# RetNet attention with a SwiGLU FFN on one core: first FFN products placed between two head pairs, and the chain of states read from PSUM

## The chip, the cores and the metric

The kernel runs on one core of a Trainium2 chip. The metric is the device time in microseconds (us). TensorE is called PE, its weight load PEld, VectorE DVE, ScalarE ACT, GpSimd POOL, SyncE SP.

## The reference

For 8 batches, 8 heads, 576 positions and a head size of 64, in fp32:

```python
scores = scale * np.matmul(q, k.transpose(0, 1, 3, 2))
Dmat = np.where(rel >= 0, gamma[:, None, None] ** rel[None, :, :], 0.0)
attn = np.matmul(scores * Dmat[None], v)                      # retention, one gamma per head
x = attn.transpose(0, 2, 1, 3).reshape(B * S, H * D)          # 4608 x 512
g = x @ w_gate;  val = x @ w_val                              # 512 x 1536
out = (g * (1.0 / (1.0 + np.exp(-g))) * val) @ w_out          # 1536 x 512
```

## The kernel before, in words

**Pairs.** The attention is worked off in 32 pairs of heads: 8 batches of 4 pairs (`HP` = 4). A pair's sequence is cut in 9 chunks of 64 positions. Retention is computed in the chunked way: inside a chunk by scores and a mask, across chunks by a state of 64 x 64 that is decayed and added to. The parts of a pair, with their lines before the change:

- `transposes` (L459): q and k turned so that PE can use them; by PE for pairs 0 to 3 (L471, L476), by DVE for the others (L489).
- `scores` (L561): products of k and q inside a chunk, L566 for the last chunk, L572 for the others, into PSUM. Pairs 0 to 3 put the last chunk's scores into bankE, the others into `sr`.
- `new_states` (L536): each chunk's own k-v products, L542, into PSUM `z`. Half `z[:, 0]` is for the even chunks, `z[:, 1]` for the odd.
- `masked` (L575): ACT copies `z[:, 0]` to `even` in SBUF (L583). DVE masks the scores (`own` L579, `last` L588). Then come the states, on DVE: `pairs` (L593) joins two chunks, `odd` (L598) is a chain of three steps in which each needs the one before, `evens` (L603) fills the states between.
- `own_values` (L523, products L531) and `earlier_values` (L545, products L554 and L558): scores times v and state times q, into PSUM `outer`.
- `to_x` (L608): DVE applies the last decay and writes the pair's quarter of x (L624, L648).

`scores` and `z` share the two banks of the tile `inner`.

**Order.** The order of every engine is written out by hand; the program is not rescheduled. For the first batch, `tick(t)` at t = 0 to 5 (L675 to L698) starts pair t, does scores and states of pair t - 1 and values of pair t - 2. Work on DVE and ACT of a pair is put in `pieces`, and `go_on` releases it.

**First tile.** The FFN's first tile has 512 tokens; its 12 blocks f of 128 hidden columns are made by `up0(f, chunks)` (L756, products L761, one gate and one value product for each quarter c of x, into bankA and bankB for even f, bankC and bankE for odd f). The weights come from HBM as 8-byte numbers and are turned into fp32 by `split` on ACT (L404, L405) and `rounding` on DVE (L418, L419). Each `rounding(j)` starts `split(j + 1)`, and some splits start the load of a later weight (`load_w`, L385 and L387; from the sixth on through ACT's queue). Before the change, ticks 4 and 5 are followed by `up0` for f = 0 and 1: quarters 0 and 1 after tick 4, quarters 2 and 3 after tick 5 (L1083 to L1085).

**Later tiles.** The other four tiles have 1,024 tokens and use sums and differences of blocks by a written table, so that fewer products are needed: `up_step` (L976, products L992) and `down_step` (L1030, products L1039). Their sums are spread over DVE and POOL: `reads` (L929) takes results out of the banks and sums them, `add` (L795) makes sums of x, of weights and of hidden blocks, L1013 to L1020 are the SwiGLU. Four banks take turns. Pairs 4 to 31 are done between these products: `tick` queues their DVE and ACT work as pieces, and every step releases one.

Of the kernel before, what the change touches and what calls it, by code (L numbers as in the profile page):

```python
# [17 lines left out]
ALU = mybir.AluOpType  # L18
# [136 lines left out]
def kernel(  # L155
# [32 lines left out]
    nc = tc.nc  # L188
# [5 lines left out]
    HP = H // 2  # L194
    L = D
    NC = S // L
    NFULL = S // P
# [29 lines left out]
    z = inner[:, :, 256:512].rearrange("p r (c d) -> p r c d", d=D)  # L227
# [21 lines left out]
    at = [4096 + 512 * i for i in range(4)] + [x0_at + 512 * i for i in range(4)]  # L249
# [14 lines left out]
    def whole(i):  # L264

        return i < needed(2) - 2
# [67 lines left out]
    step = tab[:, 2 * H : 2 * H + 2 * HP]  # L334
# [35 lines left out]
    halves = [(i, f) for f in range(2) for i in order[0:2]] + [(i, f) for i in order[2:] for f in range(2)]  # L370
# [18 lines left out]
    def bits_of(i, f):  # L389

        if i < NUP:
            return raws[i].rearrange("p c (f m two) -> p f c m two", f=2, two=2)[:, f]
        return raws[i].rearrange("p (f c) (d m two) -> p f (c d) m two", f=2, m=P, two=2)[:, f]

    def split(j):

        i, f = halves[j]  # L400
        bits = bits_of(i, f)
        top, ulp = [rest[:, part_at + 512 * (2 * n + j % 2) : part_at + 512 * (2 * n + j % 2 + 1)] for n in range(2)]
        blocks = lambda a: a.rearrange("p (c m) -> p c m", m=P)
        nc.scalar.activation(out=blocks(top), in_=bits[:, :, :, 1].bitcast(F32), func=AF.Prelu, scale=2.0 ** -112, alpha=2.0 ** 32)  # L404
        nc.scalar.activation(out=blocks(ulp.bitcast(I32)), in_=bits[:, :, :, 0].bitcast(U32), func=AF.Copy, scale=2.0 ** -29)  # L405
        parts[j] = top.bitcast(I32), ulp.bitcast(I32)
        m = j - 2 if 1 < j < 4 else j // 2
        if f and m != RAWS and m + RAWS + (m < RAWS) < len(order):
            load_w(m + RAWS + (m < RAWS))

    def rounding(j):

        i, f = halves[j]
        dst = weights[i][1][f].bitcast(I32)
        top, ulp = parts.pop(j)
        nc.vector.tensor_scalar(out=dst, in0=top, scalar1=3, scalar2=None, op0=ALU.logical_shift_left)  # L418
        nc.vector.tensor_tensor(out=dst, in0=dst, in1=ulp, op=ALU.add)  # L419
        if j + 1 < len(halves):  # L420
            split(j + 1)

    for f in range(2):
# [7 lines left out]
    even = const.tile([P, NFULL, D], F32, name="even")  # L431
# [8 lines left out]
    def places(i):  # L440
        return other if i < HP and i % 2 else (ret, ret_last, state)

    def last_scores(i):
        return bankE[:, 0:L] if i < HP else sr
# [10 lines left out]
    def vector(i):  # L455

        return i == 0
# [78 lines left out]
    def new_states(i):  # L536
        s = st[i]
        for c in range(NFULL):
            for r in range(2):
                for hl in range(2):  # L540
                    rows, at = chunk(i, hl, 2 * c + r)
                    nc.tensor.matmul(z[half[hl], r, c], s["kn"][chunk(i, hl, 2 * c + r, i < HP)], s["v"][rows, at],  # L542
                                     start=True, stop=True, skip_group_check=True)
# [31 lines left out]
    def masked(i):  # L575
        p, sr, (ret, ret_last, state) = i % HP, last_scores(i), places(i)

        def own():
            nc.vector.tensor_tensor(out=ret, in0=sc, in1=near[:, 2 * p : 2 * p + 2].unsqueeze(2).to_broadcast([P, 2, NFULL, L]),  # L579
                                    op=ALU.mult)  # L580

        def copies():
            (nc.vector.tensor_copy if vector(i + 1) else nc.scalar.copy)(out=even, in_=z[:, 0])  # L583

        odd_states = state[:, 1:].rearrange("p (c r) d -> p c r d", r=2)[:, :, 1]

        def last():
            nc.vector.tensor_tensor(out=ret_last, in0=sr, in1=last_near[:, p], op=ALU.mult)  # L588

        def pairs():  # L590

            at = odd_states
            nc.vector.scalar_tensor_tensor(out=at, in0=even, scalar=step[:, p : p + 1], in1=z[:, 1], op0=ALU.mult, op1=ALU.add)  # L593

        def odd():
            at = odd_states
            for c in range(1, NFULL):
                nc.vector.scalar_tensor_tensor(out=at[:, c], in0=at[:, c - 1], scalar=step[:, HP + p : HP + p + 1],  # L598
                                               in1=at[:, c], op0=ALU.mult, op1=ALU.add)

        def evens():
            at = state[:, 0 : NC - 1].rearrange("p (c r) d -> p c r d", r=2)
            nc.vector.scalar_tensor_tensor(out=at[:, :, 1], in0=at[:, :, 0], scalar=step[:, p : p + 1], in1=even,  # L603
                                           op0=ALU.mult, op1=ALU.add)

        return [copies, own, [last, pairs, odd, evens]]

    def to_x(i):  # L608
# [66 lines left out]
    def tick(t, lo=HP, hi=NP, spread=False, then=None):  # L675
        go_on(len(pieces))
        if hi == HP:

            if lo <= t - 1 < hi:
                scores(t - 1, True)  # L680
                new_states(t - 1)
                pieces.extend(masked(t - 1))
                go_on(3)
            if lo <= t - 2 < hi:
                own_values(t - 2)
            for f in transposes(t) if lo <= t < hi else ():
                f()
            if t + 1 == HP:
                split(0)
            if lo <= t - 2 < hi:  # L690
                earlier_values(t - 2)
                if t == HP:
                    rounding(2)
                    rounding(3)
                to_x(t - 2)[0]()
            if t + 1 == HP:
                rounding(0)
            return  # L698
        if lo <= t - 2 < hi:
            own_values(t - 2)  # L700
        if lo <= t - 1 < hi:
            new_states(t - 1)
        if lo <= t - 2 < hi:
            earlier_values(t - 2)
        if lo <= t - 1 < hi:
            scores(t - 1, t - 2 < lo)
        if lo <= t - 1 < hi and whole(t - 2) and not whole(t - 1):
            decay(slice(0, H), slice(0, H), half[1])
        copies, *masks = masked(t - 1) if lo <= t - 1 < hi else (lambda: None,)
        keys, *new = transposes(t) if lo <= t < hi else (lambda: None,)  # L710
        outputs = to_x(t - 2)[0] if lo <= t - 2 < hi else lambda: None
        late = needed(1) - 4 <= t < needed(1) - 2 or light(t - 2)
        if late and masks:
            own, (last, pairs, odd, evens) = masks
            pieces.extend([lambda: (copies(), own(), last(), outputs()), [pairs, odd, lambda: (evens(), keys())]])
        elif late:
            pieces.append(lambda: (copies(), outputs(), keys()))
        else:
            pieces.extend([lambda: (copies(), keys()), outputs])
            for own, (last, pairs, *rest_of) in [masks] if masks else []:  # L720
                pieces.extend([own, [lambda: (last(), pairs()), *rest_of]])
        if then and new:
            pieces.extend(new[:-1])
            pieces.append(lambda: (new[-1](), then()))
        else:
            pieces.extend(new)
            pieces.extend([then] if then else [])
        if not spread:
            go_on(len(pieces))
# [8 lines left out]
    def go_on(n):  # L738
        for _ in range(min(n, len(pieces))):
            while part_on():  # L740
                pass
# [14 lines left out]
    def up0(f, chunks):  # L756

        pair = banks[2 * (f % 2) : 2 * (f % 2) + 2]
        for gv, bank in enumerate(pair):
            for c in chunks:  # L760
                nc.tensor.matmul(bank, w_up[:, f // 4, gv, f % 4, c // 2, (c % 2) * P : (c % 2 + 1) * P], xs[0][:, c, :],  # L761
                                 start=(c == 0), stop=(c == HP - 1))
        if HP - 1 in chunks:
            s = io[:, (f % 2) * T0 : (f % 2 + 1) * T0]
            nc.scalar.activation(out=s, in_=pair[0], func=AF.Silu)
            nc.vector.tensor_tensor(out=hid0[f], in0=pair[1], in1=s, op=ALU.mult)
# [41 lines left out]
    for line in OUT_SUMS:  # L808
        i, s = line.split("|")
# [266 lines left out]
    for t in range(HP + 2):  # L1076
        tick(t, 0, HP)

        if t == 3:
            load(HP)  # L1080
        for j in {3: (1,), 5: (4, 5)}.get(t, ()):
            rounding(j)
        for f in range(2):  # L1083
            if t > 3:
                up0(f, range(2) if t == 4 else range(2, HP))  # L1085
    load(HP + 1)


# [116 lines left out]
```

## Time and profile before

| what | value |
|---|---|
| median of three runs (lowest, highest) | 1046.8 us (1046.59, 1056.34) |
| the profiled execution's own time | 1047.18 us |
| its span | 1045.5 us |
| busy: PE / PEld / DVE / ACT / POOL | 1027.6 / 843.9 / 653.9 / 297.2 / 401.9 us |
| DVE chain steps L598, 96 of them: min / median / max | 0.271 / 0.285 / 1.853 us |
| pair 2's values begin on PE (L531) | 27.65 us |
| last product of blocks 0 and 1 begins / block 2 begins on PE | 45.41 / 45.84 us |

A timeline line gives the start in us from the span's start, the length in us, the engine, the line of the kernel, operation and tiles, and in brackets the idle time before it with what ended it. A line of waits gives who waited for whom: us in total, times, longest. A line on a source line gives the number of instructions and the shortest, median and longest duration in ns. A line of windows gives a stretch, then its length and each engine's busy time, and at the end the granted clock of PE, the share of the DMA engines and GB/s.

### The profile page before, as it was taken

To read this page: it belongs to the slowest core of one execution; us is meant where nothing else is said; L and a number is where in the kernel's file an instruction comes from. 1 tells how busy PE (TensorE), PEld (TensorE's weight loads), DVE (VectorE), ACT (ScalarE), POOL (GpSimd) and SP (SyncE) were. 2 spreads that over 40 slices of the span, in tenths; PEclk is the share of its full clock that TensorE was granted. 3 is DMA by queue.
4 is the path that set the end of the run, shared out by engine and by line. 5 is a ranking of instruction groups with operands and counts; after the bars stand their busy time and mean duration, and the time that the engine had idled before them with its cause. 6 is when DMAs were issued, how large, how long until landed. Compare 5 with 4: busy or idle time off the path is not lost.

```text
span 1045.5 us, 21496 instructions
## 1 busy us (share of the span) xinstructions
PE 1027.6 (98%) x8448; PEld 843.9 (81%) x8448; DVE 653.9 (63%) x1063; ACT 297.2 (28%) x646; POOL 401.9 (38%) x347
## 2 busy tenths in 40 slices
PE   7999999999999999999999999999999999999998
PEld 6444555888888888888888888888888888888887
DVE  4678878777769757555357786535476644344644
ACT  3466423243533222232322102223120022231110
POOL 2002367767476035612223048312250483222505
PEclk9999999999999999999999999999999999999999
DMA  9999867776678887665676777545554565555653
GB/s 248 242 283 258 198 197 267 207 212 182 186 204 227 239 249 200 193 178 149 176 220 159 214 182 220 154 136 155 154 174 140 153 200 152 152 153 161 181 161 101
DMA packets 310380, 199.10 MB, mean 190 GB/s; under 512 B 220168, under 2 KB 254984, under 8 KB 310280
## 3 DMA queue, kind: packets, MB, share of 16 engines
q1 hardware_dynamic: 279000, 161.51, 57.2%
q10 hardware_dynamic: 31280, 36.22, 10.4%
q8 instruction: 67, 1.10, 0.5%
q14 instruction: 33, 0.27, 0.1%
HBM read 157.56 MB, written 40.11 MB: 189 GB/s over the span
## 4 chain that ended last, share of the span: by engine, by line
PE 76%; DVE 4%; DMA 1%; ACT 0%; issue 0%; POOL 0%; ACTq 0%; DVEq 0%
PE bankC L992 12%; PE bankE L992 12%; PE bankA L992 11%; PE bankB L992 11%; PE bankA L1039 6%; PE bankB L1039 6%; PE bankC L1039 6%; PE bankE L1039 6%; DVE rest L929 1%; PE outer L531 1%; PE inner L572 1%; DVE state L598 1%; PE outer L558 1%; PE inner L542 1%; DVE arena L1016 1%
## 5 line engine op out<-in xcount | busy, mean ns | idle before, releaser
L929 POOL TENSOR_TENSOR rest<-rest 128x512 f32<-128x512 f32 x65 | 92.1, 1421 | 296.7 <-DVE rest L929 277.9
L1013 ACT ACTIVATE io<-rest 128x256 f32<-128x256 f32 x180 | 74.9, 416 | 305.3 <-DVE rest L929 259.1
L992 PE MATMUL bankA<-rest,arena 128*128 128x256 f32 x544 | 128.9, 380 | 1.8 <-DVE rest L929 1.0
L992 PE MATMUL bankC<-rest,arena 128*128 128x256 f32 x544 | 129.2, 380 | 1.4 <-DVE rest L929 1.4
L795 POOL TENSOR_TENSOR arena<-arena 128x512 f32<-128x512 f32 (+1 forms) x72 | 112.5, 1574 | 38.3 <-DMA up<-arena 22.4
L992 PE MATMUL bankE<-rest,arena 128*128 128x256 f32 x512 | 121.4, 380 | 1.0 <-DVE rest L929 1.0
L992 PE MATMUL bankB<-rest,arena 128*128 128x256 f32 x512 | 121.2, 379 | 0.0
L992 PEld LDWEIGHTS bankA<-rest,arena 128*128 128x128 f32 x544 | 103.0, 190 | 16.9 <-issue 1.9
L1020 POOL TENSOR_TENSOR arena<-rest,io 128x256 f32<-128x256 f32 x72 | 52.1, 729 | 167.3 <-ACT io L1013 167.3
L992 PEld LDWEIGHTS bankC<-rest,arena 128*128 128x128 f32 x544 | 102.8, 190 | 16.3 <-issue 1.8
L992 PEld LDWEIGHTS bankE<-rest,arena 128*128 128x128 f32 x512 | 97.0, 190 | 14.7 <-DVE rest L929 1.4
L992 PEld LDWEIGHTS bankB<-rest,arena 128*128 128x128 f32 x512 | 97.0, 190 | 13.4 <-issue 0.2
L795 POOL TENSOR_TENSOR rest<-rest 128x256 f32<-128x256 f32 (+1 forms) x66 | 67.8, 1048 | 100.9 <-DVE rest L419 61.2
L929 DVE TENSOR_TENSOR rest<-bankB,rest 128x512 f32<-128x512 f32 x72 | 48.8, 686 | 65.6 <-PE bankB L992 49.7
L929 DVE TENSOR_TENSOR rest<-bankC,rest 128x512 f32<-128x512 f32 x72 | 48.9, 687 | 64.6 <-PE bankC L992 45.9
L929 DVE TENSOR_TENSOR rest<-bankA,rest 128x512 f32<-128x512 f32 x72 | 48.8, 685 | 61.1 <-PE bankA L992 43.5
L929 DVE TENSOR_TENSOR rest<-bankE,rest 128x512 f32<-128x512 f32 x71 | 48.2, 687 | 60.5 <-PE bankE L992 46.1
L1016 DVE SCALAR_TENSOR_TENSOR arena<-rest,io 128x256 f32<-128x256 f32 x84 | 57.8, 689 | 11.1 <-ACT io L1013 10.9
L1039 PE MATMUL bankC<-arena 128*128 128x256 f32 x252 | 58.4, 381 | 0.3 <-issue 0.3
L1039 PE MATMUL bankB<-arena 128*128 128x256 f32 x252 | 58.3, 381 | 0.0
L1039 PE MATMUL bankA<-arena 128*128 128x256 f32 x252 | 58.0, 380 | 0.2 <-DVE arena L795 0.2
L1039 PE MATMUL bankE<-arena 128*128 128x256 f32 x252 | 57.9, 379 | 0.0
(189 smaller groups left out, 1632.4 us busy)
## 6 DMA issues: line engine op xcount, KB each, us to landing
arena<-up SPq DMA_DIRECT2D x234, 256.0 KB, 2.7
arena<-dn SPq DMA_DIRECT2D x104, 384.0 KB, 3.9
up<-arena ACTq DMA_DIRECT2D x78, 256.0 KB, 4.1
dn<-rest SPq DMA_DIRECT2D x78, 128.0 KB, 1.9
out_dram<-rest SPq DMA_DIRECT2D x31, 256.0 KB, 3.7
qk<-in_q_dram SPq DMA_DIRECT2D x108, 72.0 KB, 2.4
qk<-in_k_dram SPq DMA_DIRECT2D x108, 72.0 KB, 3.1
rest<-in_moe_w_out_dram ACTq DMA_DIRECT2D x6, 1024.0 KB, 5.4
```

The source lines that it names most:

```text
L531: m = nc.tensor.matmul(value(i, hl, c), s["v"][rows, at], ret[rows, c % 2 if whole(i) else hl, c // 2], start=start, stop=start, skip_grou ...
L542: nc.tensor.matmul(z[half[hl], r, c], s["kn"][chunk(i, hl, 2 * c + r, i < HP)], s["v"][rows, at], start=True, stop=True, skip_group_check= ...
L558: nc.tensor.matmul(xr[half[hl]] if c + 1 == NC else value(i, hl, c), state[half[hl], c, :], s["qT"][half[hl], column(i, hl, c)], start=Fal ...
L572: nc.tensor.matmul(sc[chunk(i, hl, 2 * c + r)[0], r if whole(i) else hl, c], kT[half[hl], at], qT[half[hl], at], start=True, stop=True, sk ...
L598: nc.vector.scalar_tensor_tensor(out=at[:, c], in0=at[:, c - 1], scalar=step[:, HP + p : HP + p + 1], in1=at[:, c], op0=ALU.mult, op1=ALU.add)
L795: eng.tensor_tensor(out=dst, in0=srcs[0], in1=srcs[1], op=ALU.add if op[0] == "add" else ALU.subtract)
L929: eng.tensor_tensor(out=at(op[1]), in0=at(op[2]), in1=at(op[3]), op=ALU.add if op[0] == "add" else ALU.subtract)
L992: m = nc.tensor.matmul(b[:, gv * TB : (gv + 1) * TB], w[:, gv, ts(c, P)], rhs[:, c, :], start=(opens and gv == 0 and c == 0), stop=(c == 1 ...
L1013: nc.scalar.activation(out=s, in_=src[:, 0:TB], func=AF.Silu, scale=-1.0 if negative else 1.0)
L1016: return lambda: nc.vector.scalar_tensor_tensor(out=dst, in0=src[:, TB : 2 * TB], scalar=-1.0, in1=s, op0=ALU.mult, op1=ALU.mult)
L1020: nc.gpsimd.tensor_tensor(out=dst, in0=src[:, TB : 2 * TB], in1=s, op=ALU.mult)
L1039: nc.tensor.matmul(b[:, m * TB : (m + 1) * TB], lhs[:, qd, ts(m, P)], w[:, qd], start=(opens and qd == 0 and m == 0), stop=(qd == NQ - 1), ...
```

## The change

Two things are changed. In the first batch, `tick(4)` no longer begins with scores and states of pair 3. It begins with the values of pair 2; then come block 0's products on quarters 0 and 1, pair 2's way into x, roundings 2 and 3 (the latter without starting split 4), then scores and states of pair 3, split 4, and block 1's products on quarters 0 and 1. After tick 5 both blocks take quarter 2 first, and then both take quarter 3.

For pairs 4 to 31 the chain of states reads PSUM: `pairs` writes only the first joined state to SBUF and joins the other three in place in `z[:, 1]`; `odd` takes its second input from `z[:, 1]`, and `evens` takes it from `z[:, 0]` in place of `even`. Pairs 0 to 3 keep the old form.

```diff
-    def rounding(j):
+    def rounding(j, ahead=True):
...
-        if j + 1 < len(halves):
+        if ahead and j + 1 < len(halves):
             split(j + 1)
...
+        firsts, summed = (NFULL, odd_states) if i < HP else (1, z[:, 1])
...
         def pairs():
-            at = odd_states
-            nc.vector.scalar_tensor_tensor(out=at, in0=even, scalar=step[:, p : p + 1], in1=z[:, 1], op0=ALU.mult, op1=ALU.add)
+            for at, c in ((odd_states[:, :firsts], slice(0, firsts)), (summed[:, firsts:], slice(firsts, NFULL))):
+                if firsts < NFULL or c.start == 0:
+                    nc.vector.scalar_tensor_tensor(out=at, in0=even[:, c], scalar=step[:, p : p + 1], in1=z[:, 1, c],
+                                                   op0=ALU.mult, op1=ALU.add)
         def odd():
             at = odd_states
             for c in range(1, NFULL):
                 nc.vector.scalar_tensor_tensor(out=at[:, c], in0=at[:, c - 1], scalar=step[:, HP + p : HP + p + 1],
-                                               in1=at[:, c], op0=ALU.mult, op1=ALU.add)
+                                               in1=summed[:, c], op0=ALU.mult, op1=ALU.add)
         def evens():
             at = state[:, 0 : NC - 1].rearrange("p (c r) d -> p c r d", r=2)
-            nc.vector.scalar_tensor_tensor(out=at[:, :, 1], in0=at[:, :, 0], scalar=step[:, p : p + 1], in1=even,
+            nc.vector.scalar_tensor_tensor(out=at[:, :, 1], in0=at[:, :, 0], scalar=step[:, p : p + 1], in1=even if i < HP else z[:, 0],
                                            op0=ALU.mult, op1=ALU.add)
...
-            if lo <= t - 1 < hi:
+            def new_pair():
                 scores(t - 1, True)
                 new_states(t - 1)
                 pieces.extend(masked(t - 1))
                 go_on(3)
+            if lo < t < hi:
+                new_pair()
             if lo <= t - 2 < hi:
                 own_values(t - 2)
...
                 earlier_values(t - 2)
                 if t == HP:
-                    rounding(2)
-                    rounding(3)
+                    up0(0, range(2))
                 to_x(t - 2)[0]()
+            if t == HP:
+                rounding(2)
+                rounding(3, False)
+                new_pair()
+                split(4)
+                up0(1, range(2))
...
+    for c in range(2, HP):
         for f in range(2):
-            if t > 3:
-                up0(f, range(2) if t == 4 else range(2, HP))
+            up0(f, [c])
```

## The prediction

> **What bounds the kernel now.** I read the page's busy shares first, then the list of waits by engine, then the timelines at the places that this list names, and last the durations of the lines that the diff edits.
>
> ```profile
> PE 1027.6 (98%) x8448; PEld 843.9 (81%) x8448; DVE 653.9 (63%) x1063; ACT 297.2 (28%) x646; POOL 401.9 (38%) x347
> q8 instruction: 67, 1.10, 0.5%
> ```
>
> TensorE (PE) is busy for 98% of the span. No PE product is added or removed, so all that the change can win or lose at first hand is time in which PE stands still. The waits of PE, in us (total, times, longest), those that this change can touch:
>
> ```profile
> PE bankC L476 <- issue: 1.7, 1, 1.7
> PE bankC L992 <- DVE rest L929: 1.4, 1, 1.4
> PE bankA L992 <- DVE rest L929: 1.0, 1, 1.0
> PE bankA L761 <- DVE rest L624: 0.5, 1, 0.5
> PE outer L531 <- DVE arena L418: 0.4, 1, 0.4
> ```
>
> Two groups. L476, L531 and L761 lie in the first 46 us, where the order is changed. The two L992 waits lie at 269 and 324 us, in the first full FFN tile. Nothing above 2 us is to be had at one place.
>
> The early stretch, timeline of PE and DVE (start, length, work, idle before):
>
> ```profile
> 21.49 0.27 PE L476 MATMUL bankC<-ident,rest 64*64 64x64 f32 x1
> 23.41 0.39 PE L476 MATMUL bankC<-ident,rest 64*64 64x64 f32 x6 [1.65 <-issue]
> ...
> 25.52 1.28 DVE L624 TENSOR_TENSOR rest<-outer,tab 128x256 f32<-128x256 f32 x3
> 27.65 1.01 PE L531 MATMUL outer<-ret,v 64*64 64x64 f32 x32 [0.38 <-DVE arena L418]
> ```
>
> The stop at 21.76 to 23.41 is in the middle of one group of products, with no wait of the program. The PE instructions from 23.41 to 27.65 number 254, and two of its sequencer: 256. A packet of the instruction queue is 1.10 MB / 67 = 16.4 KB, and 16,896 PE instructions over 66 packets are 256 each. The packets begin at 20.76 and 25.07 us, and each stop ends 2.6 us after such a start. I read both stops as PE waiting for its own next instructions while short 64x64 products use them up; the name DVE L418 at the second is then not the cause (what pair 2's values need of DVE, the last L624, ends at 26.80). The clock answers to the first stop:
>
> ```profile
> 23.75:27.16 3.41, 3.41 (x123) 3.33 (x117) 1.72 (x5) 2.69 (x6) 0.45 (x1) 0.50 1.08 284
> ```
>
> Column PEclk is 0.50 there and 1.00 around it. Last, the two later waits, DVE's timeline ahead of each, and the durations of the chain's line:
>
> ```profile
> 264.33 0.68 DVE L929 TENSOR_TENSOR rest<-bankB,rest 128x512 f32<-128x512 f32 x1
> 264.93 2.75 DVE L598 SCALAR_TENSOR_TENSOR state<-state,tab 128x64 f32<-128x64 f32 x3
> 267.61 1.27 DVE L929 TENSOR_TENSOR rest<-bankA,rest 128x512 f32<-128x512 f32 x2
> ```
>
> ```profile
> 319.05 3.29 DVE L598 SCALAR_TENSOR_TENSOR state<-state,tab 128x64 f32<-128x64 f32 x3
> 322.27 1.28 DVE L929 TENSOR_TENSOR rest<-bankC,rest 128x512 f32<-128x512 f32 x2
> ```
>
> ```profile
> L598 DVE SCALAR_TENSOR_TENSOR state<-state,tab x90: 271/285/1853, 11.9 to 778.6; 128x64 f32<-128x64 f32 x90
> ```
>
> Three chain steps of 0.285 us median (0.93 us together when undisturbed) take 2.75 and 3.29 us, and the readings of the banks, queued behind them on DVE, come late: PE stands until each is done. POOL runs an L795 or L963 operation under each slow step.
>
> **What the Trainium skill says.** "SBUF — State Buffer", section "Who interferes with whom": a VectorE instruction with two SBUF inputs contends with a GpSimd instruction that reads SBUF, one with at most one SBUF input outside the two-port modes does not. The trace agrees: L598, both inputs in SBUF, ranges from 271 to 1853 ns; L593, whose second input is in PSUM, from 465 to 472 ns over 30. "TensorE: Matmul & The Clock Gate", section "Part 1: The HAM clock gate (the "warmup" mystery)": the PE clock is halved after an idle window of about 3.4 us and restored after a busy one; windows are free-running. The trace agrees, with one half-clock window of 3.41 us after a stop of 1.65 us.
>
> **The change part by part.**
>
> (a) Chain of states, 28 pairs (i >= 4); pairs 0 to 3 keep their instructions. Removed: SBUF as second input of L598 and L603. Added: one DVE instruction a pair, since L593 (0.47 us at 256 columns) becomes one of 64 columns to SBUF and one of 192 that writes PSUM in place. By columns between the rows of 64 (0.285) and 256 (0.471): 0.285 + 0.41 = 0.69, so +0.22 us of DVE a pair, 28 x 0.22 = 6.2 us. No row of before shows DVE writing PSUM: between 0 and 0.5 us a pair; I take 0.22, and what hides it is DVE's idle 37%. Saved: the L598 steps that are above 0.38 us sum to 18 us of excess over 0.285; DVE is some 12 us less busy. On PE's path only two excesses count. At 264.93 the excess is 1.8 us, less 0.2 added: PE's 1.04 us vanish. At 319.05 it is 2.4 us: PE's 1.44 us vanish. Sum -2.48. What is late next: at 274.4 PE waits 0.51 us for kT (DVE L489); DVE comes about 1.6 us earlier there and PE 1.04, so this wait does not grow; I book no gain.
> New wait: the products L542 of the next pair overwrite z, which now is held until the last step (evens) rather than until pairs. Behind L542 on PE stand the earlier values, L558, which wait for the same evens in before too, and no PE wait at L558 or L542 is listed: cost 0; if that cover fails, L542's 0.5 us a pair is exposed.
>
> (b) First batch. Scores and states of pair 3 (L566, L572, L542; 136 instructions, 25.3 to 27.26, 1.95 us at the low clock) leave the place ahead of pair 2's values. So PE now reaches these values at 25.4 and waits for the last L624: start at 26.9, instead of 27.65 in before (-0.75). The instruction limit is no longer in the way: values of pair 2 are also 136 instructions, so the fetched block's edge falls behind them. Then: values of pair 2; block 0's four products (8 x 0.43 = 3.45); pair 3's scores and states, 1.1 at full clock (60 rows of the same kind in 1.2 at 59.66); block 1's four products, 3.45; values of pair 3, 1.5; eight products in quarters, 8 x 0.86 = 6.87.
> At full clock: 26.9 + 1.5 + 3.45 + 1.1 + 3.45 + 1.5 + 6.87 = 44.8, before 45.84: -1.0.
> But PE is now idle for 1.5 of the 3.41 us of the window 23.75:27.16, much as in the window before, which had 52% of work and was followed by the half clock. If the half clock stays to 30.58, values of pair 2 take 2.2 (to 29.1), and of the block's 3.45 only 0.74 is done by 30.58, so it ends at 33.3; the rest adds to 46.2: +0.35. Both ends: -1.0 and +0.35. I take +0.3, since the trace's own 52% window went to the half clock.
> DVE in this order: to_x(1) to 26.8, roundings 0 and 1 to 29.27, to_x(2) to 30.8, roundings 2 and 3 to 33.2, then pair 3's mask, last, pairs, chain, evens (2.5 us) after PE's 33.0 to 34.4. Block 1's second bank (bankE) must wait for `last`, which reads it: done 1.2 us after the states, while bankC's products take 1.72. The values of pair 3 need evens about 3.1 us after the states, and PE reaches L558 5 us after. Third-quarter products need to_x(2) only; the fourth, 3.4 us later, needs to_x(3), 1.5 us: PE's 0.47 us at L761 vanishes, as counted. Splits 4 and 5 on ACT stand behind the copy of pair 3's states, so the one weight load that ACT issues at 34.84 goes out 1 to 2.5 us later; ACT uses that slot at 58.4, and roundings are 5 us ahead of PE (done 54.5, used at 59.7): cost 0. The queues of SP and POOL keep their order.
>
> Sum: +0.3 - 2.5 = -2.2 against the profiled execution's 1047.18 us (span 1045.5 and 1.7 around it): 1045.0. That execution is 0.4 above the median of the runs, 1046.8, so I forecast **1044.6**.
>
> **The rivals.**
> 1. *Given back.* POOL's locks strike other DVE work of two SBUF inputs (L795, L929, L1016, which I saw at 1.4 to 2.0 us), or PE waits at kT instead; the first batch comes out at +0.75 more because the release at 27.65 was a true wait for DVE. For: 1.0 us of PE idle at 192.84 has such an L795 of 1.75 us. Against: those stay as they were. Half of (a), and +1.0: 1046.8 - 1.2 + 1.0 = 1046.6.
> 2. *More.* The clock comes back early (-1.0 in place of +0.3) and the 0.5 at kT goes: 1044.6 - 1.3 - 0.5 = 1042.8.
> 3. *Slower.* Steps that read and write PSUM are slow, or z held longer stops PE's L542 once a pair. From 0.09 us a pair on PE (2.5 / 28) the gain is gone; at the full 0.5 us, 28 x 0.5 - 2.2 = +11.8: 1058.6. Against: L593 with a PSUM input costs 0.471, L603 without one 0.479, and L558's cover.
> 4. *It does nothing:* the locked steps were late anyway, PE's waits stay with other names: 1046.8 + 0.3 = 1047.1.
>
> **How the numbers follow.** Forecast 0.55 (own range 1043.6 to 1045.7), rival 1 0.20, rival 2 0.12, rival 3 0.06, rival 4 0.07. About 1%, 10.5 us, is what a measurement of this kernel can tell from no change. The range 1041.8 to 1047.4 holds the first two rivals, the fourth and the forecast, and leaves out most of rival 3 and tails. Only rival 3 at its full price passes 1%: slower 0.03; nothing known makes 10 us of gain: faster 0.02; same 0.95.
>
> **What would show it.** Right: chain steps all near 0.28 us with no long ones; no PE wait near 269 and 324; L531 of pair 2 at 26.9 behind a named DVE L624; PE reaching f = 2 between 44.8 and 46.2. Wrong: PE waits at L542 or L558 for DVE; an in-place step over 0.6 us; new PE waits of over 1 us at L992.

## The result, and the profile after

The changed kernel takes 1043.54 us (median of 20 runs, 1040.74 to 1048.88), beside 1047.6 us for the kernel before in the same measurement (20 runs, 1044.41 to 1056.34). The medians are 4.1 us apart. The ratio worked out from all the runs is 0.9957, 95% interval 0.9942 to 0.9972, which is 4.5 us less, between 2.9 and 6.1. The forecast was 1044.6 us, 2.2 us less. The profiled execution of the changed kernel is a short one: its own time is 1040.84 us, its span 1039.1 us.

The first part of the profile's page, busy time by engine:

```profile
PE 1025.6 (99%) x8448; PEld 843.2 (81%) x8448; DVE 642.3 (62%) x1091; ACT 297.4 (29%) x646; POOL 400.5 (39%) x347
```

DVE has 28 instructions more and is 11.6 us less busy. The largest waits of PE, as listed for before:

```profile
PE outer L531 <- DVE rest L627: 1.8, 2, 1.5
PE bankE L1003 <- DVE rest L940: 0.9, 1, 0.9
...
PE bankA L772 <- issue: 0.4, 1, 0.4
```

(L1003 is before's L992, L772 its L761, L940 its L929.) Both waits of 1.0 and 1.4 us for a bank that L929 had not yet read are gone, and so are the wait of 0.5 us at kT and the stop at L476. A wait of 1.5 us at L531 is new. DVE's timeline at the place of the 3.29 us chain, and the durations of the chain's lines:

```profile
315.02 0.68 DVE L940 TENSOR_TENSOR rest<-bankB,rest 128x512 f32<-128x512 f32 x1
315.62 0.90 DVE L601 SCALAR_TENSOR_TENSOR state<-state,tab,inner 128x64 f32<-128x64 f32 x3
316.44 1.28 DVE L940 TENSOR_TENSOR rest<-bankC,rest 128x512 f32<-128x512 f32 x2
```

```profile
L595 DVE SCALAR_TENSOR_TENSOR inner<-even,tab,inner x28: 422/423/423, 61.3 to 769.0; 128x192 f32<-128x192 f32 x28
```

```profile
L601 DVE SCALAR_TENSOR_TENSOR state<-state,tab,inner x84: 269/281/283, 61.8 to 770.1; 128x64 f32<-128x64 f32 x84
```

The chain takes 0.90 us where it took 3.29. Of its 84 steps with an input in PSUM none is over 283 ns. POOL still works under it:

```profile
315.55 1.27 POOL L974 TENSOR_TENSOR arena<-arena 128x512 f32<-128x512 f32 x1
```

What held the steps before is seen by laying POOL's timeline of the kernel before beside the chain:

```profile
319.23 1.27 POOL L963 TENSOR_TENSOR arena<-arena 128x512 f32<-128x512 f32 x1
320.45 1.81 POOL L795 TENSOR_TENSOR arena<-arena 128x768 f32<-128x768 f32 x1
```

The two long steps begin at 319.39 and 320.62 and last 1.19 and 1.73 us, 0.9 and 1.4 us more than the median. They end at 320.58 and 322.35, each 0.08 us after one of these operations. This is so throughout. In the profile of the kernel before, 21 steps of the chain begin under a TENSOR_TENSOR of POOL (two tensor inputs) that has more than 0.32 us to go, and all 21 end 0.08 us after it. But 7 steps begin under a TENSOR_SCALAR of POOL (one tensor input), and all 7 end before it does. Over the fourteen profiles that are compared below, it is 175 of 175 steps with both inputs in SBUF under the one kind, and 0 of 79 under the other. In the changed kernel 22 of the 84 steps with a PSUM input begin under a TENSOR_TENSOR, and none is held. A chain of the kernel before, and the POOL operation under its last two steps, which take 0.40 and 0.28 us:

```profile
162.80 1.04 DVE L598 SCALAR_TENSOR_TENSOR state<-state,tab 128x64 f32<-128x64 f32 x3
163.05 0.85 POOL L793 TENSOR_SCALAR rest<-rest 128x256 f32<-128x256 f32 x1
```

The Trainium skill's "SBUF — State Buffer", "Who interferes with whom", says that a VectorE instruction with two SBUF inputs contends with a GpSimd instruction that reads SBUF. These traces agree for GpSimd's two-input operations, and do not show it for the one-input ones.

### The profile page after: what moved, and what is told of

The parts are those of the page before. It is cut to its first block, busy times and chain, and to the rows that moved or that the text cites. A ratio compares the mean times of both kernels' runs of the same rounds, so it can differ in the third digit from the quotient of the medians.

```text
span 1039.1 us, 21528 instructions
## 1 busy us (share of the span) xinstructions
PE 1025.6 (99%) x8448; PEld 843.2 (81%) x8448; DVE 642.3 (62%) x1091; ACT 297.4 (29%) x646; POOL 400.5 (39%) x347
## 4 chain that ended last, share of the span: by engine, by line
PE 78%; DVE 2%; issue 1%; ACT 0%; DVEq 0%
PE bankC L1003 13%; PE bankE L1003 13%; PE bankB L1003 13%; PE bankA L1003 13%; PE bankB L1050 6%; PE bankC L1050 6%; PE bankA L1050 6%; PE bankE L1050 6%; PE outer L531 1%; PE inner L572 1%; PE outer L558 1%; PE inner L542 1%; DVE rest L806 1%; DVE arena L806 0%; DVE rest L940 0%
## 5 line engine op out<-in xcount | busy, mean ns | idle before, releaser
L940 POOL TENSOR_TENSOR rest<-rest 128x512 f32<-128x512 f32 x65 | 91.6, 1414 | 299.1 <-DVE rest L940 279.8
L1003 PE MATMUL bankC<-rest,arena 128*128 128x256 f32 x544 | 129.1, 380 | 0.0
L1003 PE MATMUL bankA<-rest,arena 128*128 128x256 f32 x544 | 128.7, 379 | 0.0
L1003 PE MATMUL bankE<-rest,arena 128*128 128x256 f32 x512 | 121.4, 380 | 0.9 <-DVE rest L940 0.9
L1003 PE MATMUL bankB<-rest,arena 128*128 128x256 f32 x512 | 121.2, 379 | 0.0
L1003 PEld LDWEIGHTS bankA<-rest,arena 128*128 128x128 f32 x544 | 103.2, 190 | 14.5 <-issue 0.5
L1003 PEld LDWEIGHTS bankC<-rest,arena 128*128 128x128 f32 x544 | 102.9, 190 | 14.6 <-POOL arena L806 0.3
L1003 PEld LDWEIGHTS bankE<-rest,arena 128*128 128x128 f32 x512 | 96.9, 190 | 14.6 <-DVE rest L940 1.4
L1003 PEld LDWEIGHTS bankB<-rest,arena 128*128 128x128 f32 x512 | 97.1, 190 | 13.3
L940 DVE TENSOR_TENSOR rest<-bankB,rest 128x512 f32<-128x512 f32 x72 | 48.9, 687 | 67.4 <-PE bankB L1003 51.5
L940 DVE TENSOR_TENSOR rest<-bankC,rest 128x512 f32<-128x512 f32 x72 | 48.9, 687 | 65.8 <-PE bankC L1003 47.1
L940 DVE TENSOR_TENSOR rest<-bankA,rest 128x512 f32<-128x512 f32 x72 | 48.9, 687 | 61.5 <-PE bankA L1003 44.1
L940 DVE TENSOR_TENSOR rest<-bankE,rest 128x512 f32<-128x512 f32 x71 | 48.2, 687 | 60.0 <-PE bankE L1003 46.7
```

Source lines behind the costliest of these rows:

```text
L940: eng.tensor_tensor(out=at(op[1]), in0=at(op[2]), in1=at(op[3]), op=ALU.add if op[0] == "add" else ALU.subtract)
L1003: m = nc.tensor.matmul(b[:, gv * TB : (gv + 1) * TB], w[:, gv, ts(c, P)], rhs[:, c, :], start=(opens and gv == 0 and c == 0), stop=(c == 1 ...
```

## The experiments

Each stands with what was expected of it before it ran. Ratios are to the kernel before in the same measurement, with the 95% interval.

**The order alone** (the changed kernel with `masked` as before):

```diff
-        firsts, summed = (NFULL, odd_states) if i < HP else (1, z[:, 1])
...
-                                               in1=summed[:, c], op0=ALU.mult, op1=ALU.add)
+                                               in1=at[:, c], op0=ALU.mult, op1=ALU.add)
...
```

> Only the order of the first batch is changed; the chain of states is that of before. My theory (the order is worth 0 to 2 us, the chain the rest): ratio to before between 0.998 and 1.000; block 2 begins on PE at 44.0 to 46.2 us; the long L598 steps of up to 1.8 us and PE waits of 1.0 to 1.4 us behind them near 265 and 320 us are still there. Rival (the order carries the whole gain): ratio about 0.996, and PE's later waits are not larger than in the changed kernel.

Measured: 1.0006 (0.9992 to 1.0021). The later waits of PE are all there:

```profile
PE bankC L999 <- DVE rest L936: 2.1, 1, 2.1
PE outer L531 <- DVE rest L623: 1.9, 2, 1.5
PE outer L558 <- DVE state L602: 1.6, 1, 1.6
PE inner L542 <- ACT kn L506: 1.3, 2, 1.1
PE bankA L999 <- DVE rest L936: 1.3, 1, 1.3
```

Block 2 begins at 41.77 us, earlier than both ends of the expectation, and yet nothing is left at the end. The order does not carry the gain.

**The chain alone** (the kernel before with the new `masked`):

> Only the chain of states is changed; the first batch has the order of before. My theory: all chain steps near 0.28 us, no PE wait near 265 and 320 us, ratio 0.996 to 0.998 (2.5 to 4 us). Block 2 begins at 45.8 us as in before if the half clock and PE's stop at 21.8 us come in every execution; near 44 us if they come only in some. Rival (the order carries the gain): ratio 0.999 to 1.001.

Measured: 0.9945 (0.9926 to 0.9965), 5.8 us less. No PE wait near 265 or 320 us. It carries the whole gain. The gain is larger than expected (0.9945 against 0.996 to 0.998), and above the prediction's 2.5 us for the chain even at the interval's end of 3.7.

**The same instructions, but the chain's second input in SBUF** (chain alone, with the joined states written in place into `even`). It asks whether the memory of this one input is what counts:

```diff
-        firsts, summed = (NFULL, odd_states) if i < HP else (1, z[:, 1])
+        firsts, summed = (NFULL, odd_states) if i < HP else (1, even)
```

> First batch as in before. Pairs 4 to 31 have the split joining and evens from PSUM as in the changed kernel, but the three joined states are written in place into the SBUF tile even, so that each chain step again has two SBUF inputs. My theory [...]: long steps of 0.6 to 1.9 us come back, PE waits of about 1 us behind them too, ratio 0.999 to 1.002. Rival (the split, or another length of the steps, or z being used longer makes the gain): steps near 0.28 us and ratio 0.996 to 0.998.

Measured: 0.9997 (0.9981 to 1.0014). DVE's timeline at the same chain, and two of PE's waits:

```profile
320.29 3.24 DVE L602 SCALAR_TENSOR_TENSOR state<-state,tab,even 128x64 f32<-128x64 f32 x3
323.46 1.27 DVE L933 TENSOR_TENSOR rest<-bankC,rest 128x512 f32<-128x512 f32 x2
```

```profile
PE bankC L996 <- DVE rest L933: 1.5, 1, 1.5
PE bankA L996 <- DVE rest L933: 1.0, 1, 1.0
```

This kernel has the split, the in-place write and the evens from PSUM, and only lacks the PSUM input of the three steps. Without it the held steps are back (27 over 0.4 us, up to 1.85), and the whole gain is gone. So the gain comes from the memory of this one input; that `evens` reads PSUM is not what saves the time.

**Empty instructions ahead of the first transposition:**

> The kernel before, with 64 empty instructions for TensorE ahead of its first transposition, where it waits 4 us for data anyway. My theory (PE's stops in the first 30 us are at the edges of fetched blocks of 256 of its instructions): the stops move 64 instructions up in the program: the one at 27.65 us no longer stands at the first L531 of pair 2 but inside pair 3's scores or states (L572 or L542), and the one at 21.8 us no longer in the transposition of the last chunks (L476) but in L471 or L531 ahead of it. Rival (a wait for DVE or ACT): both stay at the same products.

This told nothing of its question: the program that was built holds 21,496 instructions as before, so the empty ones had been left out. It serves as a second execution of the kernel before: stops at L476 (0.2 us) and L531 (2.1 us), 1043.8 us in its single run.

**Real instructions ahead of it** (the same, with 16 products into a corner of PSUM that nothing reads):

```diff
+    for _ in range(16):
+        nc.tensor.matmul(outer[half[0], 1, 384 : 384 + L], ident[half[0], half[0]], ident[half[0], half[0]],
+                         start=True, stop=True, skip_group_check=True)
     for t in range(HP + 2):
         tick(t, 0, HP)
```

> The kernel before with 16 small products (64 instructions of PE) into an unused corner of PSUM ahead of the first transposition, where PE waits for data. My theory (PE stops at the edges of blocks of 256 of its instructions until the next block is fetched): the stops move 64 instructions up in the program, from L476 of pair 3 to pair 2's states or the first L531 of pair 1, and from the first L531 of pair 2 to the first L542 of pair 3, and each ends 1.3 to 1.6 us after a packet of the instruction queue does. Rival (a wait for DVE): the wait stays at the first L531 of pair 2.

PE's timeline:

```profile
19.97 0.28 PE L542 MATMUL inner<-v,rest 64*64 64x64 f32 x3 [0.82 <-issue]
...
25.34 0.69 PE L542 MATMUL inner<-v,rest 64*64 64x64 f32 x32 [1.97 <-issue]
25.86 1.33 PE L531 MATMUL outer<-ret,v 64*64 64x64 f32 x32
```

Both stops are at the products named, 64 instructions further up in the program, and the L531 of pair 2 no longer waits. The packets of the instruction queue end at 18.58 and 24.20 us, 1.4 and 1.1 us ahead; the second is a little under the span on record. (The one run of this kernel took 1052.5 us; with other stops in it, its time is not compared.) At the edges where before, after, chain_sbuf and nops_first stop, PE goes on 1.35 to 1.6 us after a packet's end. PE stops for its own instructions there; the name that the list of waits gave, DVE L418, was not the cause.

**The changed kernel again, and two variants** measured beside it:

> The changed kernel as it is, a second measurement beside the next two. If the chain carries all of the gain and the order none: ratio to before 0.994 to 0.997, the same as the kernel with the chain alone. If the order has a cost or a gain of its own: apart from that kernel's 0.9945 by more than 0.002.

Measured: 0.9956 (0.9941 to 0.9972), as the first time and as the chain alone.

The chain alone with only the quarter order of the diff:

```diff
-            if t > 3:
-                up0(f, range(2) if t == 4 else range(2, HP))
+            if t == 4:
+                up0(f, range(2))
+    for c in range(2, HP):
+        for f in range(2):
+            up0(f, [c])
```

> The new chain, the order of before, and of the new order only that blocks 0 and 1 both take quarter 2 before they take quarter 3. PE's wait of 0.47 us at L761 for the last quarter of x goes; nothing else changes. Ratio 0.994 to 0.996; 0.5 us is below what the runs can tell, so the profile decides: no wait at the up0 products of quarter 3, block 2 0.5 us earlier after the same start of pair 2's values.

Measured: 0.9961 (0.9946 to 0.9976). The wait of 0.47 us at quarter 3 is gone. Block 2 begins at 46.53, because PE's stop at L531 was 3.1 us in this execution, and the clock was halved for 6.83 us from 25.99 us on. So the half microsecond can't be read off block 2's start.

Pair 4's keys on GpSimd, in the changed kernel (`1 < i <= HP` for `1 < i < HP` in `keys`):

> The changed kernel with one thing moved: the keys of pair 4 are scaled by GpSimd in place of ScalarE. Theory A (the early time that the order wins is lost at pair 4's states, L542, which wait for the scaled keys, queued on ScalarE behind splits that wait for a weight from HBM): no wait at L542 of pair 4, block 4 begins 8.2 us after block 3 also where block 3 begins before 49 us, ratio up to 0.002 below that of the changed kernel. Theory B (the order wins nothing early, or the weight load itself is the limit): PE waits at a block's product for a rounding instead, block 4 not before 59 us, ratio that of the changed kernel.

Measured: 0.996 (0.9942 to 0.9978). No wait at L542, but block 3 began at 50.59 us, so the case that it was meant for did not come up. The run doesn't tell theory A from B.

**Where the order's early time goes.** In the profile of the changed kernel taken again, PE stands 2.16 us at L558. DVE's timeline ahead of it, then PE's:

```profile
163.78 0.88 DVE L806 TENSOR_TENSOR rest<-rest 128x256 f32<-128x256 f32 x1 [3.77 <-DMA dn<-rest]
164.59 0.27 DVE L595 SCALAR_TENSOR_TENSOR state<-even,tab,inner 128x64 f32<-128x64 f32 x1
```

```profile
166.71 1.13 PE L558 MATMUL outer<-qT,state 64*64 64x64 f32 x32 [2.16 <-DVE state L606]
```

The states stand on DVE behind a sum that waits for its buffer to be stored. Four kernels try this, with two mends: the states ahead of the sums, and the keys as above. They are the changed kernel with the first mend alone, the changed kernel with both, the order alone with both, and the kernel before with both as the measure for the last. The first mend, in the changed kernel:

```diff
             tick(tick_at[m], HP, FIRST, tick_at[m] + 1 < needed(1))
-            go_on(1)
+            go_on(2)
```

> The changed kernel, but while the first tile's down products run, pairs 10 to 12 have their states (joining, chain, evens) on VectorE ahead of the sums of down weights that stood between the mask and them. Theory A (the stop of 1.6 to 2.2 us at L558 near 165 us, seen in two of four executions with the new order, is these states waiting behind a sum whose buffer is still being stored): no PE wait at L558 there in any execution, no half-clock window near 166 us, median 0.5 to 1.5 us below that of the changed kernel. Theory B (the stop comes from the transfers, wherever the states stand): PE waits near 165 us as before, same ratio as the changed kernel's 0.9956.

The first mend alone measured 0.995 (0.9932 to 0.9968). No wait at L558, but PE now waits twice near 190 us, 0.9 and 1.0 us, where the changed kernel waited once. Its time cannot be told from the changed kernel's.

> As the last, and pair 4's keys scaled by GpSimd. If the order wins some 2.4 us in the first 45 us and loses them at pair 4's states and at 165 us: ratio 0.993 to 0.995, block 4 begins 8.2 us after block 3, no PE wait at L558. If not: 0.9956 as the changed kernel.

Both mends in the changed kernel: 0.9965 (0.9951 to 0.9978). Not faster; the expectation of 0.993 to 0.995 fails.

> The order of the first batch alone with the old chain, and the two mends (states ahead of the sums, pair 4's keys on GpSimd). If the order's early gain is real and was lost at these two places: ratio to the next kernel about 0.998 (2 us), to before 0.997 to 0.999. If the order wins nothing: the same time as the next kernel.

The order alone with both mends: 0.9996 (0.9981 to 1.0011).

> The kernel before with the same two mends, the measure for the last. The mends are for stops that executions of the order of before did not show: ratio 0.999 to 1.001.

The kernel before with both mends: 0.9995 (0.9978 to 1.0012). So with the two places mended the order still gains nothing, and my account of where its early time was lost is too narrow. The profile of the order with both mends shows a third place. ACT's timeline, then DVE's, then PE's waits:

```profile
54.54 0.67 ACT L404 ACTIVATE rest<-rest 128x512 f32<-128x512 f32 x1 [10.39 <-DMA rest<-in_moe_w_gate_dram]
```

```profile
55.24 0.43 DVE L418 TENSOR_SCALAR arena<-rest 128x512 int32<-128x512 int32 x1 [8.96 <-ACT rest L404]
...
60.44 0.73 DVE L489 STREAM_TRANSPOSE kT<-qk 128x576 f32<-128x576 f32 x1
```

```profile
PE outer L566 <- DVE kT L489: 4.1, 2, 3.6
```

ACT waits for a weight from HBM until 54.5 us. Splits, rounding and, behind them on DVE, pair 4's transposition wait for it, and PE's scores wait for that.

## Why the prediction was right, and where its sum was off

To see where each part's time comes from, the fourteen profiled executions are cut at four places on PE, with the lines named as in the kernel before. Each column is the length, in us, of the stage that ends there: the first batch with blocks 0 and 1, the rest of the first tile, the first up products of the later tiles, and all the rest.

| execution | to block 2 | to first L992 | to first L1039 | to PE's end |
|---|---|---|---|---|
| before | 45.8 | 130.2 | 151.1 | 714.4 |
| nops_first | 43.1 | 130.2 | 151.1 | 713.9 |
| edges | 45.1 | 132.7 | 156.1 | 713.0 |
| chain_sbuf | 47.8 | 130.2 | 150.5 | 713.7 |
| before_kept | 46.1 | 130.8 | 154.9 | 713.9 |
| chain_only (new chain) | 44.7 | 130.2 | 147.2 | 714.8 |
| chain_quarters (new chain) | 46.5 | 130.2 | 147.1 | 715.4 |
| order_only (new order) | 41.8 | 136.0 | 153.1 | 713.3 |
| order_kept (new order) | 43.1 | 134.0 | 152.7 | 713.9 |
| after (both) | 44.0 | 130.2 | 147.7 | 713.4 |
| after_again (both) | 42.8 | 136.4 | 148.0 | 713.7 |
| keys_pool (both) | 43.7 | 130.2 | 147.2 | 713.2 |
| states_first (both) | 42.5 | 132.1 | 149.3 | 714.5 |
| both_mended (both) | 46.1 | 130.2 | 148.1 | 714.9 |

- **Bound and places: right.** PE sets the time, and the chain's steps held by GpSimd made it stand. The third column is 152.8 on average for the seven executions with a chain in SBUF (150.5 to 156.1) and 147.8 for the seven with PSUM (147.1 to 149.3): 5.0 us, and the two ranges don't meet (4.4 us without edges, which has 16 products more and stops elsewhere).
- **Price of the chain's edit: right.** The split was put at 0.69 us and took 0.272 + 0.423; DVE's busy time was put at some 12 us less and is 11.6. The in-place write to PSUM cost what the estimate by columns gave. The wait for z, held longer, never showed: no profile of the new chain lists PE at L542 or L558 waiting for that reason. Rival 3 (slower) is out.
- **Size of the chain's gain: off by half.** The term that failed is "Sum -2.48", the two waits of PE in that stage. In the seven executions with SBUF PE stands for 3.3 to 5.5 us of the stage (mean 4.5), with PSUM for 0.5 to 2.0 (mean 1.0): 3.5 us. The two waits are 2.8 of this on average; one profile did not show that the stop near 325 us is 2.05 or 2.06 in four of the others. The wait at kT, of which I wrote "I book no gain", is 0.51 more. It is in this stage of all seven with SBUF and of none with PSUM; in the kernel before:

```profile
PE outer L566 <- DVE kT L489: 0.5, 1, 0.5
```

  The prediction's own figures gave this gain: with DVE 1.6 us earlier at kT and PE only 1.04, a wait of 0.51 us has to go, where the text concluded only that it doesn't grow. Second, the half clock was a cost that I had booked for the first batch only. Three of the seven with SBUF had windows at half clock in this stage (four windows of 3.41 us), a loss of 1.0 us on average, and none of the seven with PSUM did. Three of the four windows follow the chain's stop near 325 us. The fourth, at 193.26 us of the execution with the moved edges, follows a stop of 1.94 us behind a sum of 1.75 us on L795, which the change leaves as it was. So 0.7 of this 1.0 us can be the chain's. Two windows of that same execution after its stop behind the chain, the last column but two being the granted clock:

```profile
329.80:333.20 3.40, 3.40 (x9) 0.50 0.69 223
333.30:336.70 3.40, 3.40 (x18) 1.00 0.95 244
```

  A stop of 2.05 us, to 328.65, is followed by a window in which PE gets 9 products through where it then does 18. The last 0.5 us of the 5.0 is in pieces that were not followed up. Some 0.6 us are given back in the last column (714.3 against 713.7): in three of the seven PE now stands 1.2 to 1.7 us some 17 us into the down products, in two of them for an operand on its way, as in the chain alone:

```profile
PE bankC L1043 <- DMA arena<-dn: 1.3, 1, 1.3
```

- **The first batch: total right by luck.** The forecast was +0.3 us; the order alone measured 1.0006, or +0.6 us (-0.8 to +2.2). The instruction limit is shown, and the new stop is where its edge was put, at the start of block 0; PE's timeline of the changed kernel:

```profile
24.88 1.01 PE L531 MATMUL outer<-ret,v 64*64 64x64 f32 x32 [1.52 <-DVE rest L627]
...
26.39 0.70 PE L772 MATMUL bankA<-rest,arena 128*128 128x512 f32 x1
27.48 0.70 PE L772 MATMUL bankA<-rest,arena 128*128 128x512 f32 x1 [0.39 <-issue]
```

  The 1.5 us wait for L624 (L627 here) came as worked out, though it ends at 24.88 and not at 26.9; this execution has no stop at L476. But the half clock, which I let decide, came in six of seven executions with the order of before and in one of seven with the new one. Block 2 begins 2.2 us earlier on average (43.4 against 45.6), in the changed kernel's first profile at 43.99, outside the 44.8 to 46.2 of the prediction. The step that failed beside it is "cost 0" for the weights, which was worked out from the order of before; a PE that comes earlier meets the loads. The stage after that is 2.1 us longer on average (132.7 against 130.6), so that PE reaches the first L992 at 176.1 us against 176.2. Two errors of some 2 us cancel. The new order's losses are four executions with waits at pair 4's states and scores (two of them with the stop at L558). By block 4 the lead is down to 0.7 us (60.0 against 60.7). The split on ACT that ends its wait for a weight there begins at 50.1 to 54.5 us with the new order (mean 51.8) and at 50.6 to 54.2 with the old one (mean 52.1, six of the seven; chain_sbuf has no such wait): the weight comes no earlier when PE does. This and both mends' failure fit the weights from HBM setting the pace; no run that brings the weights earlier was made, so this cause is argued, not shown.
- **The rivals.** The 1043.54 us measured lie between the forecast and rival 2 (more, 1042.8), just below the forecast's own range of 1043.6 to 1045.7. Of rival 2's two terms the one at kT came true; the clock did come back early, but that gain was lost again. Rival 1 (given back) and rival 4 (nothing) don't fit a gain of 2.9 to 6.1 us. The 10.5 us that the prediction took for the least that runs can tell was too wide: the interval here is about 1.6 us to either side.

## What to carry to other kernels

When a short dependent chain on VectorE reads two SBUF operands while GpSimd is at work, look at the longest of its instructions, not the median: a step that a GpSimd operation holds up delays everything queued behind it. Leaving one operand in PSUM, where it already is, cost an extra instruction a pair and was worth it. A gain at the start of a kernel can be lost again: here 2.2 us won by block 2 were 0.1 at the first L992, so look at what the loads behind it wait for before counting on it.

## What the runs showed of the hardware that was not expected

Of the chain steps on VectorE with both inputs in SBUF, all 175 that began under a two-input GpSimd operation with more than 0.32 us to go were held until 0.08 us after its end. None of the 79 that began under a one-input operation was.

PE's instructions come in packets of 256 (16.4 KB). In the first 30 us runs of 64 x 64 products outran them: stops of 0.2 to 3.1 us, which the list of waits puts down to "issue" or to an engine that was long done. PE went on 1.1 to 1.6 us after the packet's end. The DMA engines' share was 1.05 to 1.19 from 20.34 to 30.5 us in the kernel before; whether it is this load that makes the packets late, no run tested.

The Trainium skill ("TensorE: Matmul & The Clock Gate", the table "Why this matters for your kernels") warns of idle gaps above some 3 us. Here ten stops of 1.6 to 2.2 us were followed by a window of 3.41 us at half clock, which costs up to 1.7 us more, and four stops of this length were not. The prediction called the trace in agreement with that page's rule of an idle window, but no window was idle: ahead of the half clock PE was busy for 31 to 53% of the 3.41 us (52% in the kernel before), and windows with 45 to 55% of work went both ways.
